# Moving the later gates' vector work in the head of a chunked mLSTM kernel

## The chip, the cores and the metric

The kernel runs on one core of a Trainium2 chip. A core has engines with instruction streams of their own: TensorE (PE in the profile; its weight loads are PEld), VectorE (DVE), ScalarE (ACT), GpSimd (POOL) and SyncE (SP), which here only issues DMAs. An engine takes its instructions strictly in the order of the program, and waits on semaphores for the others. The metric is the time of one execution on the device in microseconds; the median of the four runs of the kernel before is 528.3 us (527.99 to 534.72).

## The reference

Two blocks in a row. The first is an mLSTM cell over 4 batches, 8 heads, 768 steps and head size 40:

```
for t in range(S):
    m_new  = maximum(f[t] + m, i[t])
    f_stab = exp(f[t] + m - m_new);  i_stab = exp(i[t] - m_new);  m = m_new
    C = f_stab * C + i_stab * outer(v[t], k[t])
    n = f_stab * n + i_stab * k[t]
    y[t] = sigmoid(o[t]) * (C @ q[t]) / maximum(abs(n . q[t]), 1)
```

Its result, put together to 3072 rows of 320, goes through `h = x @ w_in` (320 to 2048), `g = h * cos(h)` and `g @ w_out` (2048 to 320). All of it is float32.

## The kernel before, in words

The 768 steps are cut into 6 chunks of 128, and a chunk of one batch (all 8 heads) is a *cell*: cells 0 to 3 are the first chunk of batches 0 to 3, cells 4 to 7 the second chunk, and so on to 23. Within a cell the recurrence is written as a masked product: `scores` (keys by queries, L453), times a matrix of decays E, then `values` (L478).

The running sums and maxima of the gates are taken along the steps before any cell can use them. For the first chunk this is `gates_first` on 128 steps. For chunks 1 to 5 together it is a set of functions on 32 rows of 640 steps, and this set is what the change moves:

- `gates_sums` (L241): one scan on VectorE, the running sums F1 of the forget gates
- `gates_less_sums` (L244 to L246): a1 = i - F1, and two small copies that set where each chunk begins
- `gates_maxima` (L249, L251): one scan on VectorE for the running maxima M1, and a DMA from GpSimd's queue that writes them to DRAM as `M_d[1]`, which the E matrices of cells 4 and later are read from
- `gates_exponents` (L254 to L257): four subtractions and additions on GpSimd
- `gates_exp` (L261, L262): two exponentials on ScalarE, and a DMA from GpSimd's queue to DRAM as `G_d`
- `gates_diagonal` (L266), `gates_turn` (L273, L274) and `gates_keep` (L279 to L282): the transposes of all this into `tab`. They stay in their places.

A cell in the head consists of: `spread` or `load_E` (the maxima, by matmul into PSUM for cells 0 and 1, by DMA for the others), `decay_exponents` (L381 in halves for cells 0 and 1; L375 and a GpSimd mask L376 for the others), `decay` (the exponential on ScalarE, L384), `turn` and `turn_out` (transposes of q and k on TensorE, L434, and their copies out, L440, L442 and L444), `scores` (L453), `weigh` (L459, scores times E on VectorE), `weigh_k` (L397 on GpSimd), `values` (L478), `normalize` (L545 to L558 on VectorE), `seam` (transposes L586 of the result, and the products L596 of keys and values), `seam_out` (L604) and `state` (L610, both on ScalarE).

For cells 0 and 1 `seam` writes its products into the PSUM bank `pw`, and `state` reads them from there. `warm(k)` (L839) issues k matmuls of zeros of 128x512 in bf16 into that same bank; they keep TensorE busy.

All the order is written out by hand in `first_cells` (the head, which is cells 0 to 3) and `both_parts` (the rest: in each slot, two units of the second block with parts of a cell between them). The tiles' buffers and the semaphores follow from that order. The weights are loaded and brought into their format within the head and the first four slots: SyncE issues the loads (L129, L170), ScalarE, VectorE and GpSimd do the conversion (`parts` and `join`, L138 to L149). `Up` (L631, L634) is the first product of the second block, L825 and L727 the second.

Of the kernel before, what the change touches and what calls it, by code (L numbers as in the profile page):

```python
# [29 lines left out]
def kernel(  # L30
# [209 lines left out]
    def gates_sums():  # L240
        nc.vector.tensor_tensor_scan(out=flat[0], data0=flat[3], data1=flat[0], initial=0.0, op0=OP.mult, op1=OP.add)  # L241

    def gates_less_sums():
        nc.vector.tensor_tensor(out=a1, in0=a1, in1=F1, op=OP.subtract)  # L244
        nc.vector.tensor_copy(out=shift[:, 0, 0:1], in_=F0[:, last])
        nc.vector.tensor_copy(out=shift[:, 1:R, 0:1], in_=F1[:, 0:R - 1, last])  # L246

    def gates_maxima():
        nc.vector.tensor_tensor_scan(out=flat[1], data0=flat[4], data1=flat[2], initial=M0[:, last],  # L249
                                     op0=OP.add, op1=OP.max)  # L250
        nc.gpsimd.dma_start(out=M_d[1], in_=flat[1])  # L251

    def gates_exponents():
        nc.gpsimd.tensor_tensor(out=m0[:, 0:1], in0=F0[:, last], in1=M0[:, last], op=OP.add)  # L254
        nc.gpsimd.tensor_tensor(out=m0[:, 1:R].unsqueeze(2), in0=F1[:, 0:R - 1, last], in1=M1[:, 0:R - 1, last], op=OP.add)
        nc.gpsimd.tensor_tensor(out=eW, in0=a1, in1=M1[:, :, last].to_broadcast([BH, R, C]), op=OP.subtract)
        nc.gpsimd.tensor_tensor(out=eG, in0=m0.unsqueeze(2).to_broadcast([BH, R, C]), in1=M1, op=OP.subtract)  # L257

    def gates_exp():
        for e in (eG, eW):  # L260
            nc.scalar.activation(out=e, in_=e, func=AF.Exp)  # L261
        nc.gpsimd.dma_start(out=G_d, in_=eG.rearrange("r c s -> r (c s)"))  # L262
# [80 lines left out]
    def load_E(n):  # L343
        c, b = divmod(n, B)
        E = p4.tile([128, H, C], FP, name="E", tag="E")
        if n not in SPREAD:
            src = M_d[0][ts(b, H)] if c == 0 else M_d[1][ts(b, H), ts(c - 1, C)]
            nc.sync.dma_start(out=E, in_=src.unsqueeze(0).to_broadcast([128, H, C]))  # L348
        Es[n] = E
# [18 lines left out]
    def cols(n, j, width):  # L368
        c, b = divmod(n, B)
        return tab[:, c, j, ts(b, H)].unsqueeze(2).to_broadcast([128, H, width])  # L370
# [12 lines left out]
    def decay(n):  # L383
        nc.scalar.activation(out=Es[n], in_=Es[n], func=AF.Exp, scale=-1.0)  # L384
# [9 lines left out]
    def weigh_k(n):  # L394
        if n < N - B:
            kw = p2.tile([128, H, D], FP, name="kw", tag="kw")
            nc.gpsimd.tensor_tensor(out=kw, in0=ks[n % NB][:, :, 0:D], in1=cols(n, 1, D), op=OP.mult)  # L397
            kws[n] = kw
# [47 lines left out]
    def scores(n):  # L446
        pool, tag = psum(n)
        qT, kT = qkT[n]
        ps = [pool.tile([128, HP, C], FP, name="ps", tag=tag) for _ in range(2)]
        for p in range(HP):  # L450
            for j in range(2):
                r = slice(64 * j, 64 * j + (64 if n < TURNED else D))
                nc.tensor.matmul(ps[j][:, p], kT[r, p], qT[r, p], start=True, stop=True)  # L453
        pss[n] = ps
# [80 lines left out]
    def normalize(n):  # L535
        c, b = divmod(n, B)
        pq, hs = heads_of[n]
        if n >= B:
            ph = hs
            hs = p1.tile([128, H, D1], FP, name="hs", tag="hs")  # L540
            nc.vector.tensor_tensor(out=hs, in0=pq, in1=cols(n, 2, D1), op=OP.mult)
            nc.vector.tensor_tensor(out=hs, in0=hs, in1=ph, op=OP.add)
        dn = p2.tile([128, H], FP, name="dn", tag="dn")

        nc.vector.scalar_tensor_tensor(out=dn, in0=hs[:, :, D], scalar=-TWO_PI, in1=least, op0=OP.mult, op1=OP.max)  # L545
        nc.vector.scalar_tensor_tensor(out=dn, in0=hs[:, :, D], scalar=TWO_PI, in1=dn, op0=OP.mult, op1=OP.max)
        nc.vector.reciprocal(out=dn, in_=dn)
        y = p1.tile([128, H, D], FP, name="y", tag="y")
        o = sig[c][:, ts(b, DM)].rearrange("t (h d) -> t h d", h=H)
        nc.vector.tensor_tensor(out=y, in0=o, in1=hs[:, :, 0:D], op=OP.mult)  # L550

        z = p1.tile([128, DM + 64], FP, name="z", tag="z")
        za = z[:, 0:NK * 128].rearrange("t (i k d) -> t k i d", i=2, k=HP)
        nc.vector.tensor_tensor(out=za, in0=y[:, :, 0:DA].rearrange("t (k i) d -> t k i d", i=2),
                                in1=dn.rearrange("t (k i) -> t k i", i=2).unsqueeze(3).to_broadcast([128, HP, 2, DA]),
                                op=OP.mult)
        shape = [128, 2, H, DL]
        nc.vector.tensor_tensor(out=z[:, NK * 128:].rearrange("t (e h d) -> t e h d", e=2, h=H),  # L558
                                in0=y[:, :, DA:D].unsqueeze(1).to_broadcast(shape),
                                in1=dn.unsqueeze(1).unsqueeze(3).to_broadcast(shape), op=OP.mult)  # L560
        ys[n] = z
# [44 lines left out]
    def state(n):  # L606
        if n < N - B:
            for j, r, s in halves(n):
                if n < B:
                    nc.scalar.copy(out=s, in_=pus[n][r])  # L610
                else:
                    nc.vector.tensor_tensor(out=s, in0=s, in1=pus[n][r], op=OP.add)
# [228 lines left out]
    def first_cells():  # L841
        nc.vector.memset(nil, 0.0)
        gates_in()
        nc.scalar.copy(out=ident_b, in_=ident)
        load(0, "qk")
        later_gates_in()
        load(1, "qk")
        load(0, "v")
        load_o(0, (0, 1))
        load(2, "qk")  # L850
        load_E(0)
        load_E(1)
        warm(7)
        gates_first()
        later_fills()
        wall_in(0, 0, pmu)
        wall_in(0, 1, psum_o())
        spread(0, 0)
        gates_first_out()
        decay_exponents_half(0, 0)  # L860
        turn(0)
        turn_out(0, False)
        gates_sums()
        spread(0, 1)
        decay_exponents_half(0, 1)
        decay(0)
        weigh_k(0)
        load_E(2)
        load(1, "v")
        load(3, "qk")  # L870
        load(2, "v")
        load_E(3)
        load_o(0, (2, 3))
        load(3, "v")
        pieces.extend(weights_in(0))
        wall_in(1, 0, psum_o())
        wall_in(1, 1, psum_o())
        gates_less_sums()
        spread(1, 0)
        decay_exponents_half(1, 0)  # L880
        scores(0)
        gates_maxima()
        turn(1)
        weigh(0)
        turn_out(1, False)
        sigmoid(0, slice(0, 2))
        spread(1, 1)
        decay_exponents_half(1, 1)
        gates_exponents()
        decay(1)  # L890
        weigh_k(1)
        values(0)
        normalize(0)
        scores(1)
        turn(2)
        turn_out(2, False)
        warm(2)
        seam(0)
        weigh(1)
        seam_out(0)  # L900
        state(0)
        load_E(B)
        load(B, "qk")
        decay_exponents(2)
        decay(2)
        weigh_k(2)
        gates_exp()
        values(1)
        outs.append((0, weights_out(0)))
        load(B, "v")  # L910
        load_o(1, (0,))
        load_E(B + 1)
        normalize(1)
        scores(2)
        turn(3)
        seam(1)
        weigh(2)
        turn_out(3)
        seam_out(1)
        decay_exponents(3)  # L920
        gates_diagonal()
        values(2)
        decay(3)
        weigh_k(3)
        state(1)
        scores(3)
        weigh(3)
        pg = gates_turn()
        warm(5)
        values(3)  # L930
        join(*parts(*pieces.pop(0)))
        sigmoid(0, slice(2, 4))
        gates_keep(*pg)
        pieces.extend(weights_in(1))
        load(B + 1)
        outs.extend((p, weights_out(p)) for p in range(1, 3))
        load_o(1, (1, 2, 3))
        normalize(2)
        warm(5)
        seam(2)  # L940
        seam_out(2)
        second = parts(*pieces.pop(0))
        normalize(3)
        warm(4)
        seam(3)
        join(*second, nc.vector)
        seam_out(3)
        join(*parts(*pieces.pop(0)), nc.vector)
        decay_exponents(B)
        load_E(B + 2)  # L950
        state(2)
        state(3)

        nc.scalar.activation(out=spot, in_=spot, func=AF.Exp)
# [216 lines left out]
```

## Time and profile before

| | |
|---|---|
| median of the runs | 528.3 us |
| the profiled execution | 528.49 us |
| its span, first to last instruction | 526.8 us |
| TensorE, matmuls | 518.1 us busy, 98% |
| VectorE | 410.1 us, 78% |
| ScalarE | 264.3 us, 50% |
| GpSimd | 207.8 us, 39% |
| the 16 DMA engines, data queue | 48.1% |
| head: first matmul of the second block (L631) | starts at 34.75 us |

The profile is of one execution. Times within it count from the first instruction. The page gives each engine's busy time, the span in 40 slices, the DMA queues, the chain of work that ended last and the costliest groups. The trace behind it answers further: the instructions in order of time in a stretch, with the idle time of their engine before them and what ended it; who waited for whom; the busy time and TensorE's granted clock in stretches.

### The profile page before, as it was taken

What the parts mean: (1) busy time and instruction counts of PE and PEld (TensorE: products, weight loads), DVE (VectorE), ACT (ScalarE), POOL (GpSimd) and SP (SyncE); (2) the same over time, 40 slices, a digit from 0 to 9 for tenths busy, and PEclk for the clock granted to TensorE, in tenths of its full rate; (3) what the DMA queues carried; (4) which work ended last, traced back from release to release, by engine and by line L of the source; (5) the groups of instructions that cost most, each with busy time, mean ns of one, the idle gap of its engine ahead of it and who ended that gap; (6) DMA issues with size and microseconds to landing.
All of it is one profiled execution on the core that took longest, in us unless ns stands there. A gap on an engine that the chain in (4) does not pass through costs nothing.

```text
span 526.8 us, 10592 instructions
## 1 busy us (share of the span) xinstructions
PE 518.1 (98%) x3855; PEld 343.5 (65%) x3855; DVE 410.1 (78%) x868; ACT 264.3 (50%) x420; POOL 207.8 (39%) x405
## 2 busy tenths in 40 slices
PE   8999989999999999999999999999999999999996
PEld 6956656665565666557566676677677676757596
DVE  6779967999989998998999998888778763425254
ACT  4799776867543537364455553366353422313210
POOL 7514241506427432041544353443543534344350
PEclk9999999999999999999999999999999999999999
DMA  9999978932472475455366535456433100000000
GB/s 137 228 215 248 220 205 190 217 84 62 112 164 69 96 158 118 114 109 120 109 140 145 121 86 111 106 132 131 107 96 73 42 14 27 1 1 26 0 27 26
DMA packets 134860, 57.80 MB, mean 110 GB/s; under 512 B 70248, under 2 KB 130872, under 8 KB 134808
## 3 DMA queue, kind: packets, MB, share of 16 engines
q1 hardware_dynamic: 134664, 56.93, 48.1%
q8 instruction: 30, 0.49, 0.4%
q0 software_dynamic: 96, 0.18, 0.2%
q14 instruction: 22, 0.18, 0.1%
q10 hardware_dynamic: 48, 0.02, 0.0%
HBM read 50.76 MB, written 6.34 MB: 108 GB/s over the span
## 4 chain that ended last, share of the span: by engine, by line
PE 85%; SPq 5%; DVE 4%; DMA 3%; ACT 1%; issue 1%; POOL 0%; DVEq 0%; ACTq 0%; POOLq 0%
PE po L727 30%; PE pup L631 30%; PE pup L634 9%; PE po L825 5%; PE hp L496 3%; PE ps L453 3%; SPq L332 3%; PE hp L490 2%; DMA bits<-in_moe_w_in_dram 2%; PE pu L596 1%; DMA bits<-in_moe_w_out_dram 1%; SPq L129 1%; SPq L348 1%; SPq L301 1%; DVE wt L148 1%
## 5 line engine op out<-in xcount | busy, mean ns | idle before, releaser
L631 PE MATMUL pup<-xT,w_in_sb 128*128 128x512 f32 x384 | 175.2, 598 | 0.4 <-ACT xT L604 0.2
L639 ACT ACTIVATE n<-pup 128x512 int32<-128x512 f32 x96 | 51.8, 590 | 148.4 <-PE pup L634 148.4
L642 DVE SCALAR_TENSOR_TENSOR n<-pup,n 128x512 f32<-128x512 f32 x96 | 63.1, 685 | 71.8 <-ACT n L639 71.5
L631 PEld LDWEIGHTS pup<-xT,w_in_sb 128*128 128x128 f32 x384 | 69.7, 190 | 73.2 <-issue 64.5
L376 POOL TENSOR_SCALAR_AFFINE_SELECT E<-E 128x1024 f32<-128x1024 f32 x19 | 20.8, 1093 | 156.5 <-DVE E L375 143.6
L727 PE MATMUL po<-T,sg 128*128 128x160 f32 x426 | 81.1, 299 | 0.0
L647 ACT ACTIVATE n<-n 128x512 f32<-128x512 f32 x96 | 59.5, 630 | 42.1 <-DVE n L642 42.1
L727 PEld LDWEIGHTS po<-T,sg 128*128 128x128 f32 x426 | 65.5, 190 | 0.0
L634 PE MATMUL pup<-xT,w_in_l 64*128 64x512 f32 x192 | 54.2, 641 | 0.0
L723 POOL TENSOR_TENSOR sg<-g 128x128 f32<-128x128 f32 x66 | 30.7, 465 | 47.1 <-PE po L727 40.6
L723 POOL TENSOR_TENSOR sg<-gg 128x128 f32<-128x128 f32 x66 | 31.9, 484 | 31.4 <-PE po L727 30.6
L384 ACT ACTIVATE E<-E 128x1024 f32<-128x1024 f32 x21 | 22.2, 1058 | 33.7 <-POOL E L376 30.6
L727 PE MATMUL po<-w_out_sb,g 128*128 128x160 f32 (+1 forms) x180 | 38.4, 341 | 0.0
L825 PE MATMUL po<-w_out_sb,g 128*128 128x320 f32 x128 | 38.3, 454 | 0.0
L634 PEld LDWEIGHTS pup<-xT,w_in_l 64*128 64x128 f32 x192 | 14.4, 184 | 36.4 <-issue 34.9
L414 DVE STREAM_TRANSPOSE t<-qs 128x512 f32<-128x512 f32 x34 | 35.0, 1107 | 0.3
L727 PEld LDWEIGHTS po<-w_out_sb,g 128*128 128x128 f32 x180 | 27.8, 189 | 10.7 <-issue 6.8
L727 PE MATMUL po<-w_out_sb,gg 128*128 128x160 f32 (+1 forms) x168 | 34.0, 329 | 0.0
L659 DVE SCALAR_TENSOR_TENSOR g<-pup,n 128x256 f32<-128x256 f32 x82 | 31.1, 416 | 2.1 <-ACT n L647 0.8
L459 DVE TENSOR_TENSOR E<-ps,E 128x512 f32<-128x512 f32 x48 | 30.7, 680 | 2.1 <-ACT E L384 2.1
L659 DVE SCALAR_TENSOR_TENSOR gg<-pup,n 128x256 f32<-128x256 f32 x78 | 29.7, 416 | 2.2 <-ACT n L647 1.4
L453 PEld LDWEIGHTS ps<-t,t 40*128 40x128 f32 (+1 forms) x384 | 25.0, 188 | 9.7 <-issue 9.2
(172 smaller groups left out, 855.2 us busy)
## 6 DMA issues: line engine op xcount, KB each, us to landing
E<-M_d SPq DMA_DIRECT2D x22, 512.0 KB
bits<-in_moe_w_in_dram SPq DMA_DIRECT2D x40, 128.0 KB
bits<-in_moe_w_out_dram SPq DMA_DIRECT2D x8, 640.0 KB
room<-G_d SPq DMA_DIRECT2D x34, 128.0 KB
ks<-in_k_dram SPq DMA_DIRECT2D x24, 160.0 KB
vs<-in_v_dram SPq DMA_DIRECT2D x24, 160.0 KB
out_dram<-o SPq DMA_DIRECT2D x18, 160.0 KB
o<-in_o_gate_dram SPq DMA_DIRECT2D x68, 40.0 KB
```

Of the source, the lines that this page charges most:

```text
L414: nc.vector.transpose(out=dst.rearrange("r p (t x) -> r p x t", x=T4), in_=src.rearrange("r p (x d) -> r p x d", x=T4)[:, :, :, 0:32])
L453: nc.tensor.matmul(ps[j][:, p], kT[r, p], qT[r, p], start=True, stop=True)
L459: nc.vector.tensor_tensor(out=w, in0=pss[n][j], in1=w, op=OP.mult)
L631: nc.tensor.matmul(pu, w_in_sb[:, i, ts(block(f2, e), 128)], x(i), start=(i == 0), stop=False)
L634: nc.tensor.matmul(pu, w_in_l[r, f2], x(NK, r), start=False, stop=True)
L639: nc.scalar.activation(out=self.n[e], in_=self.pu[e], func=AF.Copy, bias=0.25)
L642: nc.vector.scalar_tensor_tensor(out=self.n[e].bitcast(FP), in0=self.pu[e], scalar=0.25, in1=self.n[e], op0=OP.add, op1=OP.subtract)
L647: nc.scalar.activation(out=r, in_=r, func=AF.Sin, scale=TWO_PI_DOWN)
L659: nc.vector.scalar_tensor_tensor(out=gs[c, f2, s][:, ts(e, W)], in0=self.pu[e][:, ts(s, W)], scalar=TWO_PI, in1=n[:, ts(s, W)], op0=OP.mul ...
L723: engine.tensor_tensor(out=S[:, i], in0=x, in1=y, op=op)
L727: nc.tensor.matmul(out, g, w, start=start, stop=stop, skip_group_check=True)
L825: nc.tensor.matmul(po[0][b], gs[0, f // 2, f % 2][:, ts(b, C)], w_out_sb[:, f], start=(f == 0), stop=(f == NF - 1))
```

## The change

In `first_cells`, and nowhere else:

```diff
         turn_out(0, False)
-        gates_sums()
         spread(0, 1)
         decay_exponents_half(0, 1)
         decay(0)
+        gates_sums()
         weigh_k(0)
 ...
-        gates_less_sums()
         spread(1, 0)
         decay_exponents_half(1, 0)
         scores(0)
-        gates_maxima()
         turn(1)
         weigh(0)
         turn_out(1, False)
         sigmoid(0, slice(0, 2))
         spread(1, 1)
         decay_exponents_half(1, 1)
-        gates_exponents()
         decay(1)
-        weigh_k(1)
+        gates_less_sums()
         values(0)
         normalize(0)
+        gates_maxima()
+        weigh_k(1)
         scores(1)
 ...
         seam_out(0)
         state(0)
+        warm(4)
         load_E(B)
         load(B, "qk")
         decay_exponents(2)
         decay(2)
         weigh_k(2)
-        gates_exp()
+        gates_exponents()
         values(1)
 ...
         turn_out(3)
         seam_out(1)
+        gates_exp()
         decay_exponents(3)
         gates_diagonal()
```

The amount of vector, scalar and GpSimd work is the same. TensorE gets four matmuls more, `warm(4)` behind `state(0)`. On VectorE the order becomes: both halves of cell 0's exponents, the sums (L241), cell 1's first half, `weigh(0)`, cell 1's second half, the differences (L244 to L246), `normalize(0)`, the maxima (L249), `weigh(1)`. On GpSimd the DMA of the maxima (L251) and `weigh_k(1)` keep their order, and L254 to L257 come behind the mask and `weigh_k` of cell 2; the DMA of `G_d` (L262) comes ahead of cell 3's mask, as before, but behind exponentials that ScalarE now does after `seam_out(1)`.

## The prediction

> **What bounds the kernel now.** I read the page first, then the order in time of the first 36 us engine by engine, then TensorE's clock in stretches of 3.4 us.
>
> ```profile
> PE 518.1 (98%) x3855; PEld 343.5 (65%) x3855; DVE 410.1 (78%) x868; ACT 264.3 (50%) x420; POOL 207.8 (39%) x405
> ```
>
> TensorE has only 8.7 us without a matmul in the whole span. So a delay of TensorE in the head lasts to the end, unless a later wait takes it up. In the head it runs almost gapless too, but much of that is short matmuls that come just in time. ScalarE is the engine to look at around the added `warm(4)`; this is its order in time:
>
> ```profile
> 15.77 1.06 ACT L384 ACTIVATE E<-E 128x1024 f32<-128x1024 f32 x1
> 16.73 0.57 ACT L440 COPY t<-pt 128x512 f32<-128x512 f32 x1
> 17.20 0.59 ACT L444 COPY t<-pt 128x512 f32<-128x512 f32 x1
> 17.79 0.48 ACT L604 COPY xT<-pmu 128x384 f32<-128x384 f32 x1
> 18.29 0.60 ACT L610 COPY st<-pw 40x164 f32<-40x164 f32 x2
> ...
> 26.87 0.58 ACT L610 COPY st<-pw 40x164 f32<-40x164 f32 x2
> ```
>
> No idle time stands behind these lines: ScalarE is full from 12.43 (a table load) until `state(0)` (L610) ends at 18.89. From TensorE's order:
>
> ```profile
> 18.12 1.98 PE L478 MATMUL ph<-vs,E 128*128 128x41 f32 x16
> ...
> 27.50 1.24 PE L839 MATMUL pw<-nil 128*128 128x512 bf16 x5 [0.43 <-ACT st L610]
> ...
> 28.57 1.88 PE L478 MATMUL ph<-vs,E 128*128 128x41 f32 x16
> ```
>
> `values(1)` starts at 18.12, before `state(0)` is done. At 27.50 a `warm` waits for `state(1)`, which ended at 27.45, since both use `pw`; five of its matmuls take 28.57 - 27.50 = 1.07, so 0.214 each.
>
> **Step 1, cell 0's second half.** L241 (7.29, 1.47 us) leaves the place ahead of L381. That L381 then waits for `spread(0, 1)`, which TensorE ends at 7.24 + 1.06 = 8.30: it starts at 8.34, not 8.69, and `decay(0)` is 0.35 earlier. ScalarE's next work waits for TensorE's transposes until 11.30, so this is worth nothing by itself.
>
> **Step 2, weighing.** L244 to L246 (9.27 to 10.13) and L249 (1.53) leave the way of `weigh(0)`. By the durations: L241 8.92 to 10.39, L381 to 11.00, `weigh(0)` 10.93 to 12.18; before 12.19 to 13.44, so 1.26 earlier. But `values(0)` stands behind `spread(1, 1)` in TensorE's order, and that ends at 11.57 + 1.06 = 12.63 as before. So `values(0)` starts at 12.55 for 12.90: **0.35 gained** of the 1.26. `normalize(0)` starts at 14.56 for 14.91.
>
> **Step 3, maxima.** `normalize(0)` took 2.16 (14.91 to 17.07), `normalize(1)` 1.62 (20.13 to 21.75). The difference is L554, 0.95 against 0.42, under GpSimd's L397 (below). Now GpSimd stands still until L249 is done (its queue holds the DMA L251 first), so 1.62: ends 16.18. L249 then runs 16.11 to 17.64, and `weigh(1)` 17.57 to 18.84, 0.58 later than 16.99. It is hidden, by step 4.
>
> **Step 4, `warm(4)`.** Nothing in steps 1 to 3 moves ScalarE's full stretch, whose head is TensorE's `turn(1)`. So `state(0)` still ends at 18.89, while TensorE is through with `seam(0)` at about 17.83. It waits 1.1 us, starts `warm(4)` at 18.94, and `values(1)` at 18.94 + 4 x 0.214 = 19.80, for 18.12. At 1.88 us it ends at 21.68, for 20.10: **1.58 lost**. Behind it in TensorE's order stand `scores(2)`, `turn(3)`, `seam(1)`, `values(2)`; on VectorE `normalize(1)` waits for it and everything else behind that. Bounds: 0 if `state(0)` came 1.6 earlier, for which no row speaks, and 1.68.
>
> **Step 5, the exponents on GpSimd.** L254 to L257 moved away from `normalize(0)`, where they cost little. Where do they land? Cell 2's L375 ends at 18.77 + 1.21 = 19.98, the mask L376 takes 20.06 to 21.15, L397 0.72, L254 and L255 0.31, so L256 runs 22.16 to 23.42 and L257 to 24.7. `normalize(1)` starts at 21.71, and its L554 is due at 22.71, in the middle of L256; L558 would follow under L257. From VectorE's and GpSimd's order in time:
>
> ```profile
> 15.86 0.72 POOL L397 TENSOR_TENSOR kw<-ks,tab 128x320 f32<-128x320 f32 x1
> ...
> 15.91 0.95 DVE L554 TENSOR_TENSOR z<-y,dn 128x256 f32<-128x256 f32 x1
> ...
> 21.13 0.42 DVE L554 TENSOR_TENSOR z<-y,dn 128x256 f32<-128x256 f32 x1
> ...
> 21.47 0.28 DVE L558 TENSOR_TENSOR z<-y,dn 128x128 f32<-128x128 f32 x1
> ...
> 21.69 1.29 DVE L459 TENSOR_TENSOR E<-ps,E 128x512 f32<-128x512 f32 x2
> ```
>
> L554 began just behind the start of L397 and ended 0.28 after its end (16.58): it stood until GpSimd's instruction was over. L545 and L550, which read PSUM, ran at full speed under L257. And at 76.23 to 78.55 three VectorE instructions in a row (L144, L146, L148) ended 0.28, 0.28 and 0.55 after three GpSimd instructions in a row: one passes at each end. So L554 ends near 23.7, L558 near 25.0, and `weigh(2)` starts at 25.0 rather than 23.27: **1.7 more**, 3.3 behind 21.69. Bounds: 0, if L256 falls elsewhere, and 1.8, L554 held until L257 ends. I take 1.7, the row nearest in kind being L554's own.
>
> **Step 6, down the head.** `weigh(2)`, L442, L375, the mask of cell 3 and `decay(3)` (25.91) follow each other without a gap, so `decay(3)` is at 29.2. `gates_exp` and the DMA L262 now stand ahead of that mask: px of `seam(1)` done 25.4, L604 to 25.95, L261's first to 26.65, the DMA's 0.55 to about 27.5, and the mask is due at 28.0. Hidden by 0.5. `state(1)`, the weights' conversion, the sigmoid's table load, `normalize(2)` and L631 (34.75) follow ScalarE from there: all 3.3 later. The DMA of the maxima goes from 12.57 to 17.7; landing took 5.3, so 23.0, and its first reader, SP's `load_E` at 27.23, is not held. `G_d` is first read at 81.9. SP's order is the same, and its waits are on earlier DMAs.
>
> **Step 7, where it could be taken up.** At 70.62 ScalarE had waited 2.91 us for a piece of w_in, and TensorE then lost 1.80 us and its clock:
>
> ```profile
> 70.10:73.50 3.40, 3.40 (x11) 1.25 (x9) 2.00 (x5) 2.85 (x5) 0.93 (x2) 1.00 0.60 173
> 73.50:76.90 3.40, 1.60 (x24) 0.93 (x21) 2.88 (x8) 3.38 (x11) 2.06 (x3) 1.00 0.91 297
> 76.90:80.30 3.40, 3.40 (x7) 2.08 (x7) 3.08 (x6) 3.39 (x7) 2.61 (x4) 0.50 0.73 161
> ```
>
> (Stretch, its length, busy time of PE, PEld, DVE, ACT, POOL; then the granted clock.) Half speed for 3.4 us cost 1.7: the 16 matmuls of L825 from 76.66 took 6.27, and 4.57 at 89.12. Coming 3.3 later, the core would find the piece landed. But the rest of that chain is conversion work with the same GpSimd stalls: in the slot of cell 7, with no wait for a DMA, 6.80 us went by from the end of w_out's L148 (94.43) to L558's end (101.23). Here L148 ends at 68.93 + 3.3 = 72.23, so L558 at 79.03 for 75.83: **3.2 remain**, with much the same gap and clock loss. Behind 80 no wait of this size comes.
>
> A rule about this gap: the Trainium skill, "TensorE: Matmul & The Clock Gate", section on the HAM clock gate, says that the clock falls to half after at least one idle window of some 3.4 us. The row shows it fall after 1.80 us without matmuls. By the rule the gap of 1.1 us in step 4 could never cost the clock; by the row it is open, and the sum could get 1.7 more.
>
> **The sum.** 528.49 (span 526.8 and 1.7 around it) + 3.2 = 531.7 for the profiled execution; that lies 0.2 above the median, so **531.5**.
>
> **Rivals.**
> - *The head loses its clock too* (17%). TensorE idles 1.1 us near 18, 0.9 near 25 and 0.9 near 30. A stretch of 3.4 us with 0.43 idle (25.7 to 29.1) kept its clock, one with 1.80 lost it; 1.1 is between. Price up to 1.7: 533.2, slower by 0.9%.
> - *GpSimd's pair misses L554 and L558* (20%): it lands 0.6 us later or 1.3 earlier than I compute. Then only step 4 counts: 528.3 + 1.6 = 529.9.
> - *The wait for w_in takes it up* (15%), which ends not slower. If conversion after 70.62 runs without the stalls, the delay is covered up to 1.8, TensorE's gap closes, and with a gap under some 0.5 us the clock stays: 1.7 gained. 528.3 + 3.2 - 1.8 - 1.7 = 528.0, or 526.6 with step 4 alone. It decides from the point at which L554 of cell 5 ends no later than L634 plus 0.5.
> - *The change does what it moves things for* (8%): step 2's 0.35 arrives, and `state(0)` is early enough for `warm(4)` to fall into idle time: 527.9.
>
> The forecast keeps 40%. The range goes from 527.7 (the upper part of the covered cases) to 533.8 (a clock loss on top). One percent, 5.3 us, is about what a measurement of this kernel can tell from no change; slower than 533.6 needs a clock loss and a further stall, 8%; faster than 523.0 nothing explains, 1%.
>
> **What the profile after would show.** `weigh(0)` near 10.9, `values(0)` near 12.55; the maxima's L249 near 16.1; L839 near 18.94 released by ScalarE's L610; `values(1)` at 19.8; L554 and L558 of `normalize(1)` at about 1.0 and 1.3 us for 0.42 and 0.28; L631 first at 38.0 for 34.75; L586 of cell 5 near 79.0. Wrong it would be, above all, if L631 starts before 36, or if the clock's stretches of 0.5 are other than one.

## The result, and the profile after

| | before | after |
|---|---|---|
| median of the executions | 529.56 us (76, 526.49 to 534.72) | 531.63 us (50, 529.37 to 537.32) |
| the profiled execution | 528.49 us, span 526.8 | 531.90 us, span 530.2 |
| first L631 (the second block begins) | 34.75 us | 38.29 us |
| transposes L586 of cell 5 | 75.78 us | 79.22 us |

The ratio of the two is 1.0047, with a 95% interval of 1.0031 to 1.0063: the changed kernel is slower by 1.6 to 3.3 us. The forecast was 531.5. The executions of one kernel lie in groups by their granted clock: about half of those after, at a mean clock of 0.997, lie between 531.06 and 532.92, 11, at 0.999 or 1.0, between 529.4 and 531.4, and 12, at 0.984 or 0.986, between 535.8 and 537.3; of those before, 12 lie between 533.5 and 533.8. The sizes of these groups don't make the difference: at the same clock of 0.997 the median is 531.6 after (27 executions), and 529.0, 529.5 and 529.6 in the three series of the kernel before that were run with the experiments (8, 13 and 14 executions).

The page of the kernel after has TensorE as full as before:

```profile
PE 519.4 (98%) x3859; PEld 344.1 (65%) x3859; DVE 413.6 (78%) x868; ACT 264.2 (50%) x420; POOL 207.3 (39%) x405
```

VectorE's busy time grew by 3.5 us for the same 868 instructions. Of that, 0.92 is L554 and 1.06 is L558 of `normalize(1)`, which stood while GpSimd worked. ScalarE's order in time in the kernel after, to be held against its lines of before:

```profile
18.29 0.60 ACT L610 COPY st<-pw 40x164 f32<-40x164 f32 x2
21.59 1.06 ACT L384 ACTIVATE E<-E 128x1024 f32<-128x1024 f32 x1 [2.70 <-POOL E L376]
```

`state(0)` ends at 18.89, the same reading as before; but the work of this profile starts 0.25 us later (counted from the copy to `tab`, see the experiments), so it is 0.25 earlier than forecast. In TensorE's order the added `warm(4)` waits for it, and `values(1)` stands behind:

```profile
18.95 1.02 PE L839 MATMUL pw<-nil 128*128 128x512 bf16 x4 [1.04 <-ACT st L610]
19.81 1.88 PE L478 MATMUL ph<-vs,E 128*128 128x41 f32 x16
...
24.11 0.44 PE L586 MATMUL pmu<-ident,z 128*128 128x128 f32 x2 [0.31 <-DVE z L554]
25.37 0.33 PE L586 MATMUL pmu<-ident,z 128*128 128x128 f32 x1 [0.82 <-DVE z L558]
```

The last two lines are TensorE's transposes, waiting for the two instructions of VectorE that wait for GpSimd. VectorE's order, and then GpSimd's, in the same stretch:

```profile
22.71 1.34 DVE L554 TENSOR_TENSOR z<-y,dn 128x256 f32<-128x256 f32 x1
23.98 1.34 DVE L558 TENSOR_TENSOR z<-y,dn 128x128 f32<-128x128 f32 x1
25.24 1.27 DVE L459 TENSOR_TENSOR E<-ps,E 128x512 f32<-128x512 f32 x2
```

```profile
22.51 1.26 POOL L256 TENSOR_TENSOR room<-room,room 32x640 f32<-32x640 f32 x1
23.73 1.43 POOL L257 TENSOR_TENSOR room<-m,room 32x640 f32<-32x640 f32 x1
...
27.13 0.55 POOL L262 DMA_DIRECT2D G_d<-room  x1 [1.93 <-ACT room L261]
28.32 1.09 POOL L376 TENSOR_SCALAR_AFFINE_SELECT E<-E 128x1024 f32<-128x1024 f32 x1 [0.64 <-DVE E L375]
```

L554 ends at 24.05, 0.28 after L256's end; L558 at 25.31, 0.15 after L257's. The DMA of `G_d` is done at 27.69, and cell 3's mask waits for VectorE, not for it.

At cell 5 (stretch, length, busy time of PE, PEld, DVE, ACT, POOL, granted clock, DMA share, GB/s):

```profile
74.04:77.45 3.41, 3.41 (x10) 1.06 (x8) 3.20 (x6) 3.39 (x11) 2.26 (x3) 1.00 0.99 299
77.45:80.86 3.41, 1.71 (x24) 1.29 (x23) 3.27 (x9) 2.77 (x5) 1.27 (x3) 1.00 0.83 158
80.86:84.28 3.42, 3.42 (x8) 2.11 (x7) 3.32 (x8) 2.84 (x6) 1.96 (x2) 0.50 1.06 203
```

The same picture as before, 3.4 us later: 1.70 us without a matmul, then 3.4 us at half speed. Ahead of this place every L631 starts 3.53 to 3.54 us later than before, and behind it, to the end, 3.42 to 3.45: from there the two traces run in parallel.

### The profile page after: what moved, and what is told of

Its sections match the earlier page's. It is cut to its first block, busy times and chain, and to the rows that moved or that the text cites. A ratio compares the mean times of both kernels' runs of the same rounds, so it can differ in the third digit from the quotient of the medians.

```text
span 530.2 us, 10595 instructions
## 1 busy us (share of the span) xinstructions
PE 519.4 (98%) x3859; PEld 344.1 (65%) x3859; DVE 413.6 (78%) x868; ACT 264.2 (50%) x420; POOL 207.3 (39%) x405
## 4 chain that ended last, share of the span: by engine, by line
PE 86%; DVE 4%; DMA 3%; SPq 3%; POOL 1%; issue 1%; ACT 1%; POOLq 0%; DVEq 0%; ACTq 0%
PE po L727 30%; PE pup L631 30%; PE pup L634 9%; PE po L825 5%; PE hp L496 3%; PE ps L453 3%; DMA bits<-in_moe_w_in_dram 2%; PE hp L490 2%; SPq L332 1%; PE pu L596 1%; DMA qs<-in_q_dram 1%; PE pt L434 1%; DVE wt L148 0%; POOL E L376 0%; DVE wt L146 0%
## 5 line engine op out<-in xcount | busy, mean ns | idle before, releaser
L631 PE MATMUL pup<-xT,w_in_sb 128*128 128x512 f32 x384 | 175.1, 598 | 0.4 <-ACT xT L604 0.2
L631 PEld LDWEIGHTS pup<-xT,w_in_sb 128*128 128x128 f32 x384 | 69.7, 190 | 73.2 <-issue 64.5
L634 PE MATMUL pup<-xT,w_in_l 64*128 64x512 f32 x192 | 54.2, 641 | 0.0
L825 PE MATMUL po<-w_out_sb,g 128*128 128x320 f32 x128 | 38.3, 454 | 0.0
L634 PEld LDWEIGHTS pup<-xT,w_in_l 64*128 64x128 f32 x192 | 14.4, 184 | 36.4 <-issue 34.9
```

The costliest lines, as they stand in the source:

```text
L631: nc.tensor.matmul(pu, w_in_sb[:, i, ts(block(f2, e), 128)], x(i), start=(i == 0), stop=False)
L634: nc.tensor.matmul(pu, w_in_l[r, f2], x(NK, r), start=False, stop=True)
L825: nc.tensor.matmul(po[0][b], gs[0, f // 2, f % 2][:, ts(b, C)], w_out_sb[:, f], start=(f == 0), stop=(f == NF - 1))
```

## The experiments

The theory has three parts: the head is later by step 4 (`warm(4)` waits for ScalarE) and step 5 (the pair L256 and L257 holds L554 and L558), and nothing behind the head takes it up. Times of different profiles are compared from the copy to `tab` (L233), which starts at 6.42 in the profile before, 6.67 after, and between 5.81 and 7.18 in the others; differences below have that taken off. Ratios are to the kernel before on the same chip. Their intervals reach 0.9 to 2.3 us to each side, about as much as one part is expected to be worth; so it is the single profiles that price the parts, and the medians mostly leave it open.

### Each part alone

**Only `warm(4)`, in the kernel before:**

```diff
         state(0)
+        warm(4)
         load_E(B)
```

> The kernel before with nothing but warm(4) added behind state(0). Theory (warm(4) waits for state(0), and GpSimd's pair under normalize(1) costs the rest): here the pair L256, L257 still runs near 13.4 to 15.9, so only the wait counts. L839 starts near 18.95, values(1) at 19.8, normalize(1) runs 1.6 us with L554 and L558 at 0.42 and 0.28, weigh(2) at about 23.3, first L631 at 36.3 (34.75 + 1.58); time 1.6 us above the kernel before. Rival (the loss comes from the maxima put ahead of weigh(1), the warm falls into idle time): first L631 near 34.8, time as before. Rival (the warm costs its 0.86 us of TensorE work and no more): first L631 near 35.6.

TensorE's order in time:

```profile
18.68 1.02 PE L839 MATMUL pw<-nil 128*128 128x512 bf16 x4 [0.75 <-ACT st L610]
19.55 1.87 PE L478 MATMUL ph<-vs,E 128*128 128x41 f32 x16
...
28.80 0.58 PE L839 MATMUL pw<-nil 128*128 128x512 bf16 x1 [0.40 <-ACT st L610]
```

`weigh(3)` starts at 28.30 for 27.00, 1.55 later: step 4's 1.58. Then came something that no theory had. The stretches from 25.23 on:

```profile
25.23:28.64 3.41, 3.17 (x38) 2.90 (x38) 1.31 (x3) 1.42 (x3) 1.78 (x2) 1.00 0.85 210
28.64:32.05 3.41, 3.25 (x12) 2.04 (x11) 2.84 (x8) 3.36 (x5) 0.80 (x1) 0.50 1.07 235
```

The clock fell at 28.64, for 10.24 us, after a stretch in which TensorE was busy for 3.17 of 3.41 us. Its one gap of note is at its end, the beginning of the 0.40 that the last line shows. L631 came at 40.33. The median of 10 executions is 531.27 (ratio 1.0005, 0.9975 to 1.0035), from 527.7 to 529.7 in the four where the clock stayed, to 532.1 to 532.2 in the profiled one and its like. In the head the part costs what step 4 said, and the clock may go besides. In the time of the whole kernel this price isn't seen: the ratio's interval holds 1 as well as step 4's 1.6 us, and the four executions that kept their clock are hardly slower than those of the kernel before that kept it (527.4 and 528.6 in the same series).

**The changed kernel without `warm(4)`:**

```diff
         state(0)
-        warm(4)
         load_E(B)
```

> The changed kernel without warm(4). Theory: values(1) starts with the first half of weigh(1), near 18.3; normalize(1) begins near 20.2, ahead of L256 (22.5), so L554 and L558 meet the mask and weigh_k of cell 2 instead and lose some 0.4 each, weigh(2) near 22.6. Then a new wait is late: L256 and L257 end near 25.0, L261 follows, the DMA L262 stands ahead of cell 3's mask on GpSimd, so the mask starts near 26.7 (28.3 in the changed kernel, 24.8 before). First L631 near 36.6: about half of the 3.5 us remains, time 1.6 us under the changed kernel. Rival (the moves by themselves are harmless, all of the loss is the warm): first L631 near 34.8, time as before. Rival (the moves alone carry the loss): 38.3.

TensorE's order, and the stretches behind it:

```profile
18.81 1.98 PE L478 MATMUL ph<-vs,E 128*128 128x41 f32 x16 [0.45 <-DVE E L459]
...
30.02 1.64 PE L839 MATMUL pw<-nil 128*128 128x512 bf16 x5 [1.95 <-ACT st L610]
```

```profile
27.31:30.72 3.41, 1.46 (x14) 1.01 (x13) 1.20 (x2) 2.25 (x5) 1.77 (x2) 1.00 0.95 228
30.72:34.13 3.41, 3.41 (x17) 3.05 (x15) 2.76 (x9) 3.22 (x6) 1.28 (x1) 0.50 0.83 165
```

`values(1)` is 1.5 earlier than in the changed kernel, and so is `weigh(3)` (29.52), but not by the same cause. L554 and L558 now come ahead of the pair, under cell 2's mask and `weigh_k(2)`, and take 0.49 and 0.81, so `weigh(2)` (23.16) is even 2.5 earlier: of step 5's cost, too, most is gone. Then cell 3's mask starts at 27.30, right behind the DMA of `G_d` (26.73 to 27.28): step 6's cover of half a microsecond is used up, and 1.1 of the 2.5 is lost there, as was expected. What was not expected is the clock. TensorE, being earlier, waits 1.95 for ScalarE at the next `warm`, loses its clock for 6.83 us, and L631 comes at 40.09, later than with `warm(4)`. All ten executions have a clock of 0.99; median 532.33, ratio 1.0044 (1.0021 to 1.0068). In these two profiles the wait that the change adds costs the head 1.5 us and keeps the clock alive, by moving idle time away from there; in the kernel before, above, the profiled execution lost it all the same.

**`warm(4)` in a bank of its own**, so that it need not wait for `state(0)`:

```diff
-        warm(4)
+        warm(4, psum_o().rearrange("p h t -> p (h t)"))
```

> The changed kernel with warm(4) writing a PSUM bank of its own, so that it needs not wait for state(0). Theory: L839 starts straight behind seam(0), near 17.9, values(1) at 18.8 rather than 19.8. normalize(1) begins near 20.7; L554 falls under weigh_k of cell 2 and L558 before or under L256, so weigh(2) between 22.8 and 24.1; then the DMA L262 holds cell 3's mask until 26.7 at least. First L631 between 36.6 and 37.2, 1.1 to 1.7 us less than the changed kernel. Rival (the four matmuls' work is what costs, not the wait): first L631 stays near 38.3.

`weigh(2)` comes 2.55 and `weigh(3)` 1.46 earlier than in the changed kernel, as much as without `warm(4)`. Again TensorE waits then, 1.84 us until 29.16, and again the clock goes, from 28.79 for 10.24 us, so that L631 comes at 40.58 instead of the 36.6 to 37.2 expected. Median 532.43, ratio 1.0045 (1.0028 to 1.0062). What costs the head in step 4 is the wait, not the four matmuls.

**No `warm(4)`, and that later wait filled** with eight matmuls of zeros in a bank that waits for nobody:

```diff
         state(0)
-        warm(4)
 ...
         pg = gates_turn()
+        warm(8, ps_a.tile([128, HP, C], FP, name="pm", tag="a"))
         warm(5)
```

> The changed kernel without warm(4), with eight matmuls of zeros in a bank of their own between gates_turn and warm(5), where TensorE idled 1.95 us in the kernel without warm(4) just before its clock fell to half for 6.8 us. Theory (warm(4) costs its wait, but without it the idle time falls ahead of warm(5) and there it costs the clock): the head keeps its clock; weigh(3) 2.0 later than in the kernel before, first L631 near 36.8 instead of 40.1; runs at a granted clock of 0.996 to 1.0 rather than 0.99, median some 530, 2 us less than without the filling. Rival (the clock falls for another reason, such as the short matmuls of gates_turn): first L631 stays near 40, median 532.

The two lines of TensorE at that place:

```profile
27.98 1.90 PE L839 MATMUL pm<-nil 128*128 128x512 bf16 x8
30.01 1.24 PE L839 MATMUL pw<-nil 128*128 128x512 bf16 x5
```

The 1.95 us of waiting are now 1.90 of zeros, and the head keeps its clock. L631 starts at 37.25, 1.49 earlier than in the changed kernel, as expected. As in the last two kernels that is step 4 and most of step 5 together, less the time lost at the DMA of `G_d`. Median 530.88, ratio 1.0014 (0.9988 to 1.004).

**The pair at a fifth of its size.** L256, L257 and one exponential treat one of the five later chunks only; the weights of the later cells are left out for the rest.

```diff
-        nc.gpsimd.tensor_tensor(out=eW, in0=a1, in1=M1[:, :, last]..., op=OP.subtract)
-        nc.gpsimd.tensor_tensor(out=eG, in0=m0..., in1=M1, op=OP.subtract)
+        nc.gpsimd.tensor_tensor(out=eW[:, 0], in0=a1[:, 0], in1=M1[:, 0, last]..., op=OP.subtract)
+        nc.gpsimd.tensor_tensor(out=eG[:, 0], in0=m0[:, 0:1]..., in1=M1[:, 0], op=OP.subtract)
```

> The changed kernel with L256 and L257, and the second exponential of L261, on one of their five chunks only; the other four chunks are left out, so the later cells' weights are not the reference's. Theory: each of the pair falls from 1.26 to about 0.35 us, L554 and L558 lose at most 0.2 to 0.4 together instead of 2.0, weigh(2) starts near 23.6 (25.24 in the changed kernel) and the first L631 near 36.7: 1.6 us less than the changed kernel. Rival (VectorE's L554 and L558 are slow for another reason, such as the place of the tiles, and GpSimd's pair costs nothing): both stay at 1.3 and the first L631 at 38.3.

GpSimd's order, then VectorE's:

```profile
23.04 0.39 POOL L256 TENSOR_TENSOR room<-room,room 32x128 f32<-32x128 f32 x1
23.39 0.57 POOL L257 TENSOR_TENSOR room<-m,room 32x128 f32<-32x128 f32 x1
```

```profile
23.22 0.49 DVE L554 TENSOR_TENSOR z<-y,dn 128x256 f32<-128x256 f32 x1
23.64 0.48 DVE L558 TENSOR_TENSOR z<-y,dn 128x128 f32<-128x128 f32 x1
```

The two VectorE instructions shrink with the two GpSimd instructions under which they stand, though nothing of their own work changed. `weigh(2)` and L631 come 1.7 earlier than in the changed kernel, while `warm(4)` waits 1.04 as there: that is step 5's price, and the two instructions still lose 0.27 together. Median 530.71, ratio 1.0016 (0.9993 to 1.0038), which overlaps with the changed kernel's.

### Another place for the pair

The exponents directly behind the maxima, their exponential in its old place, no `warm(4)`:

```diff
         gates_maxima()
+        gates_exponents()
         weigh_k(1)
 ...
-        warm(4)
 ...
         weigh_k(2)
-        gates_exponents()
+        gates_exp()
```

> The vector moves alone: sums, differences and maxima where the change puts them, the exponents straight behind the maxima on GpSimd, gates_exp where it was before, no warm(4). Theory: L249 ends near 17.6, so L254 to L257 run 18.6 to 21.4, ahead of weigh_k(1) and cell 2's mask, which starts near 22.1 for 19.5; weigh(2) 24.3 for 21.7, cell 3's mask 27.4 for 24.8; L554 and L558 of normalize(1) at their 0.42 and 0.28 or little more. First L631 near 37.3 if the clock holds, up to 41 if not. So the place behind the mask of cell 2 is not worse than the earliest one. Rival (the exponents' place is what costs; the vector moves are free): first L631 near 35.

VectorE's order, and GpSimd's:

```profile
20.77 2.27 DVE L554 TENSOR_TENSOR z<-y,dn 128x256 f32<-128x256 f32 x1
22.97 1.17 DVE L558 TENSOR_TENSOR z<-y,dn 128x128 f32<-128x128 f32 x1
```

```profile
19.61 1.25 POOL L256 TENSOR_TENSOR room<-room,room 32x640 f32<-32x640 f32 x1
20.84 1.25 POOL L257 TENSOR_TENSOR room<-m,room 32x640 f32<-32x640 f32 x1
22.05 0.71 POOL L397 TENSOR_TENSOR kw<-ks,tab 128x320 f32<-128x320 f32 x1
22.73 1.27 POOL L376 TENSOR_SCALAR_AFFINE_SELECT E<-E 128x1024 f32<-128x1024 f32 x1
```

Here the pair delays `weigh_k(1)` and cell 2's mask, `weigh(2)` (25.12) then waits 0.98 for the exponential behind the mask, and L554 stood past the ends of L256 and L257 until 0.28 after L397's. That L554 and L558 would keep their 0.42 and 0.28 was wrong. TensorE's clock was gone from 25.05 for 17.07 us and again at 86.49, and L631 came at 44.29, where 41 was the latest expected. Median 537.86 of 4, ratio 1.0147 (1.0104 to 1.019). The changed kernel without `warm(4)`, which differs from this one only in the place of the exponents and of their exponentials, has 1.0044: behind the mask is the better place of the two, and much of the difference is the clock's (20.5 us at half speed against 6.8).

### The wait at cell 5

Ten matmuls of zeros go ahead of cell 5's transposes, in the kernel before and in the changed one:

```diff
-    def seam(n):
+    def seam(n, fill=0):
 ...
+            for _ in range(fill):
+                nc.tensor.matmul(px, nil, nil.unsqueeze(1).to_broadcast([128, NK + 1, C]), start=True, stop=True)
 ...
-            seam(n)
+            seam(n, 10 if n == B + 1 else 0)
```

> The kernel before with ten matmuls of zeros, 128x384, into px ahead of cell 5's transposes, where TensorE waits 1.80 us for L554. Theory (the stretch of half clock from 76.93 follows from that gap and costs 1.7): the wait of L586 falls under 0.4, no half-speed stretch at 77, L825 there takes 4.6 for 6.3; median 1 to 1.6 under the kernel before, ratio 0.997 to 0.998. Rival (the time lost there is given back behind it, since the weights' conversion is late anyway): gap and clock as said, but the time as before.

> The changed kernel with the same filling. Theory: the wait of 1.70 for L554 of cell 5 goes to under 0.4 and its half-speed stretch with it; 1 to 1.6 us less than the changed kernel, so still 1 to 1.5 above the kernel before, and 2 to 3.4 above the kernel before with the same filling: the head's loss is apart from this gap. Rival (the wait for w_in takes the head's delay up once the gap is closed): as the kernel before with the filling.

In both, the gap and the loss of clock near 77 to 81 are gone. In the changed kernel L554 and L558 stand as before (1.35 and 1.34), L631 starts at 38.03, and the lateness against the profile before falls from 3.3 to 1.4 us over cell 5: the head's loss is a thing of its own, and the gap does not take it up. The later cost is seen in TensorE's order in the changed kernel: four L636 (L634 in the other kernels), which took 1.13 us at 199.96, stretch from 209.14 to 211.22, since a transfer into `xT` landed too late.

```profile
209.14 1.65 PE L636 MATMUL pup<-xT,w_in_l 64*128 64x512 f32 x3
210.20 0.68 PE L453 MATMUL ps<-t,t 40*128 40x128 f32 x4
210.63 0.59 PE L636 MATMUL pup<-xT,w_in_l 64*128 64x512 f32 x1
```

That gave 0.95 of it back. In the kernel before with the filling the same four gave back 1.2 of the 1.87 won at cell 5. So in these two profiles a filled gap is worth less at the end than at its place. Medians: 529.04 in the kernel before (ratio 0.9996, 0.9967 to 1.0026), 531.05 in the changed one (1.0043, 1.0009 to 1.0077). These miss the gain of 1 to 1.6 us that was expected, but their intervals hold it, so between it and the rival of no gain they don't decide.

The profile of the first of these two, whose head is that of the kernel before line for line, showed one thing more, in VectorE's order and in GpSimd's:

```profile
7.50 2.49 DVE L241 TENSOR_TENSOR_SCAN room<-room,room 32x640 f32<-32x640 f32 x1
```

```profile
7.91 0.73 POOL L397 TENSOR_TENSOR kw<-ks,tab 128x320 f32<-128x320 f32 x1
```

The same two in the profile before:

```profile
7.29 1.47 DVE L241 TENSOR_TENSOR_SCAN room<-room,room 32x640 f32<-32x640 f32 x1
```

```profile
7.94 1.34 POOL L397 TENSOR_TENSOR kw<-ks,tab 128x320 f32<-128x320 f32 x1
```

Here the sums waited for the keys, there the keys for the sums. It costs `weigh(0)` 1.0 us (13.43 for 12.19, less 0.22 of offset), and TensorE lost its clock at 15.95. So this head has two outcomes, and the profile that the forecast was made from shows the lucky one. What sets them apart can be read: in all twelve profiles where GpSimd's memsets are in their place L397 starts between 7.91 and 8.05, while L241, in its old place, follows the copy to `tab` by 0.87, and that copy lay anywhere from 5.81 to 7.18. With the copy at 6.17 (only `warm(4)` added) and 6.42 (before) the sums took 1.47, with the copy at 6.64 they took 2.49.

### Is it that race?

Two kernels ask for it. One moves only the sums, which takes them away from `weigh_k(0)`:

```diff
-        gates_sums()
         spread(0, 1)
         decay_exponents_half(0, 1)
         decay(0)
+        gates_sums()
         weigh_k(0)
```

> The kernel before with the first edit alone: L241 behind both halves of cell 0's exponents. Theory: VectorE idles about 1.0 us ahead of L381's second half, and L241, L244 and L249 all still stand ahead of weigh(0), so weigh(0) starts 1.0 later than in the profile of before (13.2 for 12.2, counted from the same copy to tab), values(0) waits 1.2, and everything behind is 1.0 later. In exchange L241 meets no weigh_k(0) on GpSimd (it starts near 8.9, weigh_k(0) ends near 8.7) and takes 1.47 always; in the profile of the kernel before with the gap of cell 5 filled it took 2.49 under L397 and weigh(0) came 1.0 late. So the runs resemble those runs of the kernel before: at a granted clock of 0.997 near 529.5, none near 528.4; median as before, within 0.5 us. Rival (the edit gains the 0.35 that it gives decay(0)): median 0.3 to 1.3 under the kernel before.

The other leaves the sums and moves GpSimd's last memsets, so that `weigh_k(0)` is over early:

```diff
             fill(i)
+
+    def last_fills():
         for t in st:
 ...
         weigh_k(1)
+        last_fills()
         values(0)
```

> The kernel before with the eight memsets of the state and of the padding (L205, L207) behind weigh_k(1) on GpSimd, so that weigh_k(0) runs near 6.8 to 7.5 and is over when L241 runs. Theory: L241 takes 1.5 to 1.7 in every execution, weigh(0) never comes the 1.2 late that it came in the profile of the kernel before with cell 5's gap filled; the runs at a granted clock of 0.997 gather near 528.4 instead of 528.4 to 529.8; median 0.5 to 1 under the kernel before. Rival (the spread of the kernel before has another source, the DMAs): distribution and median as before.

The sums moved alone: 530.32, ratio 1.0015 (0.9983 to 1.0046). In its profile, one of the two slowest of ten executions, the second half (L381) waits 0.96 for TensorE, idle time that L241 filled before; L241 still meets the end of L397 and takes 1.66; L244 to L246 and L249 are still ahead of `weigh(0)`, which is 1.4 late, TensorE waits 1.66 for it and loses its clock twice in the head (span 533.0). A gain of the sums' new place alone doesn't show.

The memsets moved: 528.43, ratio 0.9973 (0.9947 to 0.9999), the one of thirteen intervals that lies below 1, and barely, so chance isn't excluded. Its VectorE and GpSimd (two lines are added above, so L241 is L243 and L397 is L399):

```profile
7.14 1.50 DVE L243 TENSOR_TENSOR_SCAN room<-room,room 32x640 f32<-32x640 f32 x1
```

```profile
6.58 0.72 POOL L399 TENSOR_TENSOR kw<-ks,tab 128x320 f32<-128x320 f32 x1 [0.34 <-DVE tab L235]
```

L399 is over at 7.30, both at full speed, and from there its head and its span (526.8) are those of the lucky profile before. That both stay at full speed is shown by this profile and the next kernel's (L241 1.52, L397 0.73); that it is worth time at the end rests on the one ratio.

### Put together

First, the memsets moved as above and cell 5's gap filled as above, in the kernel before. Second, the changed kernel with `warm(4)` taken out and both gaps filled, as above, and the DMA of `G_d` behind cell 3's mask:

```diff
             nc.scalar.activation(out=e, in_=e, func=AF.Exp)
+
+    def gates_out():
         nc.gpsimd.dma_start(out=G_d, in_=eG...)
 ...
         decay_exponents(3)
+        gates_out()
         gates_diagonal()
```

> The same, with the ten matmuls of zeros ahead of cell 5's transposes as well. Theory: both gains add up: granted clock 0.999 to 1.0 in most runs, median 527.0 to 527.8, ratio 0.996 to 0.998 to the kernel before. Rival (the lost clock only moves to another stretch of the head): median 528.5 to 529.

> The change's vector moves with its costs taken away: no warm(4), the eight matmuls of zeros ahead of warm(5) and the ten ahead of cell 5's transposes, and the DMA of G_d (L262) behind cell 3's mask. Theory: cell 3's mask starts with L375 and no longer waits for L262, about 1.0 earlier than without that edit (26.2 for 27.3 there, counted as there), first L631 near 36.2 (37.25 there); granted clock 0.999 to 1.0; median 528.5 to 529.3, 2.5 under the changed kernel and not clearly under the kernel before. Rival (the vector moves are a gain once their costs are off): median under 528.

The first gave 529.22 (ratio 1.0004, 0.9987 to 1.0021), the second 531.94 (1.0039, 1.0015 to 1.0063). Both keep the clock throughout, and neither is faster for it; both miss their expectations, and the first doesn't repeat the gain of the memsets alone. In the first, whose profiled execution was the slowest of its twelve, TensorE's order at cell 5, then ScalarE's (the lines are shifted by some):

```profile
76.91 1.78 PE L588 MATMUL px<-nil 128*128 128x384 bf16 x10 [2.48 <-DVE hs L543]
```

```profile
74.14 0.66 ACT L138 ACTIVATE wt<-bits 128x512 f32<-128x512 f32 x1 [5.99 <-DMA bits<-in_moe_w_in_dram]
```

The piece of w_in that came at 70.62 before came at 74.14 here, so VectorE's chain was late, and the zeros themselves waited 2.48. In the second kernel it came at 73.14, and further on TensorE lost 1.66 at 151.47, behind ScalarE's wait for an output transfer, and about 0.9 at 363, at the same kind of `pup` matmuls as above. The head of the second is still 1.3 behind that of before (L631 at 35.83, its copy to `tab` at 6.17). Its profile shows from what: `weigh(1)` is 0.4 later behind the maxima, cell 2's L375 takes 1.58 for 1.21 beside `weigh_k(1)`, and cell 3's takes 1.80 for 1.21 beside L257. So the pair no longer meets L554 and L558 but another VectorE instruction, and the vector moves cost the head 1.3 us even without the wait. That the gains don't add at the end is, in these two profiles, the later landing of transfers; how much of the medians it makes up is not shown.

## Why the prediction was right, step by step

Measured times are given as read and, in brackets, with the 0.25 us taken off by which the profile after starts later; the one in brackets is to be held against the forecast, which stands behind "for".

- **Steps 1 and 2**: `weigh(0)` at 11.17 (10.92) for 10.93; `values(0)` at 12.71 (12.46) for 12.55. Right.
- **Step 3**: `normalize(0)` took 1.62 (14.63 to 16.25), L249 started at 16.17 (15.92) for 16.11, and `weigh(1)` at 17.64 (17.39) for 17.57. Right, and hidden. Cell 2's L375 behind it took 1.58 for 1.21, beside `weigh_k(1)`, which the forecast did not see; with the earlier start that comes out even to 0.15.
- **Step 4**: the wait is there, its size was 1.34 and not 1.58. `warm(4)` at 18.95 (18.70) for 18.94; `values(1)` at 19.81 (19.56) for 19.80; `normalize(1)` at 21.72 (21.47), against 20.13 before. `state(0)` ended 0.25 earlier than forecast; ScalarE seems not to have been quite full before: L604 started 0.59 behind L444 and the first L610 0.50 behind L604, and here 0.48 and 0.37; this fits short waits for TensorE's `seam(0)`, whose two parts were done there at 17.75 and 18.19. In the kernel before alone `warm(4)` cost 1.55 of the 1.58.
- **Step 5**: L554 to 24.05 (23.80) for 23.7; L558 to 25.31 (25.06) for 25.0; `weigh(2)` at 25.24 (24.99) for 25.0. GpSimd's order sets this end, not TensorE's, so what step 4 fell short of came back here: 1.96 for 1.7, together 3.3 as forecast. The pair at a fifth gave 1.7 of it back.
- **Step 6**: cell 3's mask at 28.32, 0.6 behind the DMA, so hidden; L631 at 38.29 (38.04) for 38.0.
- **Step 7**: ScalarE no longer waits for w_in (L138 runs from 71.15 without idle time), yet L586 of cell 5 starts at 79.22 (78.97) for 79.0, and the 16 L825 behind it take 6.27 us again. Of the 3.54 us, 3.44 remain behind it.

**The sum** held for the profiled execution: 531.90 for 531.7. Between all executions the ratio gives 2.5 us (1.6 to 3.3) where the sum had 3.2, which the interval still holds. That 531.5 lies 0.1 from the median after is luck to about 1 us: it was counted from 528.3, the median of four executions, where that of 76 is 529.56, and the difference is smaller than forecast. A term that was not in the sum is a gain at the head's very beginning. The forecast took L241's 1.47 in step 1 as its price; where L241 meets `weigh_k(0)`, it took 2.49 in another profile with the same head. The changed order puts it at 9.19, while GpSimd stands still. In 5 of the 14 profiles the copy to `tab` lies at 6.64 or later, so an estimate from these rows is that the kernel before loses the race in about a third of its executions, for 0.4 us on average at most. The memsets' run puts it at 0.1 to 2.8 us, if all of that ratio is the race. Transfers that land later also cover part of a late head, so that the race makes up the whole difference is not shown.

**The rivals.** That the pair misses L554 and L558, and that the wait for w_in takes it up, did not come: the profile decides against both. (Of the latter's two sums the second comes to 526.4 by its own terms, not 526.6.) That the head loses its clock too was underpriced at 1.7. The profiled execution kept it, through a stretch (16.01 to 19.42) with 2.37 us of matmuls; but 12 of 50 executions lie 4.2 to 5.7 us above the median of those at 0.997, at the clock that a loss of 15 to 17 us at half speed would give. Of the two signs of being wrong, L631 before 36 did not come; "other than one" stretch at half speed did in many executions that were not profiled: these 12, by their mean clock, had more, and the 11 at 0.999 or 1.0 had none of 3.4 us. Where it is lost in those was not profiled. That the change does what it moves things for came in part: step 2's 0.35 arrived at `values(0)` (0.44, with the offset off), and step 4 ate it.

## What to carry to other kernels

When work is moved from one engine's crowded place, look at what runs on the *other* engine at the new place: two GpSimd instructions of 1.3 us cost VectorE 2 us and, in the profiles, the whole kernel 1.7, with no semaphore between them. A filler that writes to a bank still being read is a wait, not a filler; but before such a wait is removed, look where the idle time goes next, since the clock may be lost there. And a kernel that is tight to a few tenths should be profiled more than once before a forecast is built on it: here a race between two engines moved it by 1.0 us, and late transfers by 0.95 to 1.3.

## What the runs showed of the hardware

- VectorE instructions with two inputs in SBUF stood under GpSimd's tensor instructions: L554 0.42 alone, 0.95 under one of 0.72 us, 1.34 under one of 1.26, 0.49 under one of 0.39. The Trainium skill, "GPSIMD Engine Reference", section on the specifications, says that GpSimd shares its SBUF interfaces with VectorE and names instructions with two SBUF inputs among those that contend; the rows agree. Here the VectorE instruction lasted to the end of the GpSimd instruction and 0.15 to 0.28 more. That one passes at each end, as step 5 had it, is no rule: L554 stood past two ends and took 2.27 us.
- The waiting goes both ways: L397 took 0.73, or 1.34 when L241 had started 0.65 us ahead of it, and 1.06 with a lead of 0.93 (only `warm(4)` added); where L241 had 0.41 of a lead, it was L241 that waited (2.49).
- In these profiles the clock changed only at whole steps of 3.41 us from where it first rose. Neither the idle nor the busy time of TensorE in such a step tells whether the clock falls after it. It fell after 1.71 us of matmuls (after, cell 5), and after 3.17 (only `warm(4)` added); it stayed after 2.37 and 2.27 in the head of the changed kernel. And this stretch, in the changed kernel without `warm(4)`, kept it with hardly more matmul time than the first of these:

```profile
78.51:81.92 3.41, 1.72 (x24) 0.74 (x20) 3.27 (x8) 3.38 (x6) 1.98 (x3) 1.00 1.05 188
```

  The Trainium skill, "TensorE: Matmul & The Clock Gate", section on the HAM clock gate, has the clock fall after at least one idle window of about 3.4 us. The rows here differ: TensorE's longest idle time within any profile was 2.48 us, and the clock fell in 11 of the 14. What decides is open: the stretch with 3.17 us held 29 short matmuls on 32 or 64 rows, but a stretch of much the same work after the change (26.25 to 29.66) kept the clock.
- At half speed the clock stayed for 3.41 us or a multiple: 6.83, 10.24 and 17.07 were seen.
